# The low part of w_out's first quarter: three products moved from the pooling pass to the wait for the first chunk's softmax weights

## The chip, the core and the metric

The kernel runs on one core of one Trainium2 chip. Its time is the device time of one execution in microseconds (us): three runs of the kernel before took 1018.67, 1019.38 and 1019.65 us, median 1019.38. One more execution was taken with the hardware profiler; every duration below is from that one.

The engines: PE is TensorE's matmul (PEld its weight load), DVE is VectorE, ACT is ScalarE, POOL is GpSimd, SP is SyncE, which issues the DMAs here. Each works through its own list of instructions in the order in which the program wrote them; semaphores hold an instruction until another engine has come far enough. L130 is line 130 of the kernel.

## The reference, cut to what matters

`x` has 12480 rows of 128 channels, `inducing` 32 rows. Inputs are given as 8-byte words; weights are turned into float32 pairs on the chip.

```python
def mab(q, kv):
    s = scale * (q @ kv.T); s = s - s.max(-1)
    a = np.exp(s); a /= a.sum(-1) + 1e-9
    return a @ kv
h = mab(inducing, x)          # pooling: 32 rows attend to all 12480
z = mab(x, h)                 # every row of x attends to the 32
h1 = z @ w_in;  z2 = np.maximum(0.01 * h1, h1) @ w_out          # first feed-forward, 128 -> 2048 -> 128
h2 = z2 @ w2_in               # second feed-forward
g = where(h2 >= 1, h2, where(h2 <= -1, 0, (h2 + 1) ** 2 / 4));  y = g @ w2_out
```

## The kernel before, in words

Nothing sorts the instructions: the order of the calls in the kernel is the order on every engine, and the framework only adds the semaphores that the data and the buffers ask for.

**The pass** (lines 319 to 337) does the pooling over `x` in nine bands with a running maximum. A step `s` has on PE the scores of band `s` (L265), the transposes of the exponentials of band `s-1` (L287), and their products with `x` (L298); DVE takes the maximum (L266, L270) and adds the result up (L302, L312); ACT does the exponentials (L277, L279) and copies the transposed ones (L289). The last two bands have their transposed `x` from memory (`xl`). `warm` (L316) issues products whose results nobody reads: fillers.

**The weights** come as 8-byte words in 512-column quarters. `convert(n, q)` turns quarter `q` of weight `n` (0: w_in, 1: w_out, 2 and 3: the second pair) into float32 in a few steps: L104 on ACT and L105 on DVE, L107, L109 (with L112 on ACT, which writes the high part `whi`), L114. `work(n)` runs `n` such steps, two quarters in turn. The pair of scratch tiles `cva`, `cvb` of a conversion is taken from a pool of three pairs. The low part `wlo` of a w_out quarter is made in one of two ways: on POOL (L121, L122), or, for w_out's quarters 0 and 1 (`PE_LO = 2`), by `low_parts`: three products that add `cva` and `cvb` and subtract `whi` in a PSUM bank (L130, L131, L132), and a copy by ACT (L133). The first two of the three have float32 operands and show as two matmul records each, L132 has fp32r operands and shows as one. `lows` holds what is still to be done; until then the pair of scratch tiles cannot be given to another quarter.

Quarter 0 of w_out is done in step 6 of the pass (L335 and L336), quarter 1 at the third slot of the first chunk (L598). Both read `whi` and their scratch pair, and are wanted by the products of the first chunk (L488).

**Between pass and chunks** (lines 340 to 506) the pooling result `HT` is made (L366), and then the first chunk's attention, one chunk being 480 rows: `attend(0, 0)` scores on PE (L445), `attend(0, 1)` maximum and difference on DVE (L450, L452), 2 exponential on ACT (L455), 3 normalisation on DVE (L459 to L462), 4 the split into a high and a low part (L466 to L469), 5 transposes by products (L475), 6 the copy to `aT` (L480). With them stand `hidden(0, ...)`, which folds `HT` into w_in (L393, L397, L400: `Gs`), conversion steps, and six fillers (L502) in the wait before L475.

**The chunks** (from L509): slot `k` has the product of `aT` with 128 columns of `Gs` (L527), its high and low part (L530, L537), and the three products each with w_out of slot `k-4` (L487 to L489); later the second pair of weights runs five chunks behind. PE is all but gapless from there to the end.

Of the kernel before, what the change touches and what calls it, by code (L numbers as in the profile page):

```python
# [51 lines left out]
NS_B = len(BANDS)  # L52
# [2 lines left out]
         "c0", "w", "w", "w", "w", "w")  # L55
WARM_A = {1: 5, 2: 8}
WARM_B = 4
WARM_T = (3, 4, 4, 5, 6)
WORK_S = ((0, 0), (0, 2), (0, 3), (0, 3), (1, 3), (1, 4), (2, 4), (1, 2), (1, 2))
UNTIL_S = (0, 1, 2, 2, 3, 4, 5, 5, 6)  # L60
WORK_T = (2, 1, 2, 2)
# [7 lines left out]
def moe_kernel(ctx: ExitStack, tc, x_d, xf_d, xl_d, xt_d, it_d, w1_d, w2_d, w3_d, w4_d, y_d):  # L69
# [13 lines left out]
    bank = [ps.tile([128, 512], F32, name=f"bank{i}", tag=f"bank{i}") for i in range(8)]  # L83
# [10 lines left out]
    def convert(n, q):  # L94

        t = raws.pop((n, q))
        up, low = t[:, :, 1], t[:, :, 0]
        sl = slice(q * QW, (q + 1) * QW)  # L100
        a = cv.tile([128, QW], F32, name="cva")
        b = cv.tile([128, QW], F32, name="cvb")
        au, bu = a.bitcast(U32), b.bitcast(U32)
        nc.scalar.activation(a, up.bitcast(F32), AF.Abs, scale=WORD_SCALE)  # L104
        nc.vector.tensor_scalar(out=bu, in0=up.bitcast(U32), scalar1=0x80000000, scalar2=None, op0=ALU.bitwise_and)  # L105
        yield
        nc.vector.scalar_tensor_tensor(out=au, in0=au, scalar=3, in1=bu, op0=ALU.logical_shift_left, op1=ALU.bitwise_or)  # L107
        yield
        nc.vector.tensor_scalar(out=bu, in0=au, scalar1=0xFF800000, scalar2=None, op0=ALU.bitwise_and)  # L109
        if n:  # L110
            hi, lo = whi[n - 1][:, sl], wlo[n - 1][:, sl]
            nc.scalar.activation(hi, a, AF.Copy)  # L112
        yield
        nc.vector.scalar_tensor_tensor(out=b, in0=low.bitcast(U32), scalar=2.0 ** -52, in1=b, op0=ALU.mult, op1=ALU.mult)  # L114
        if n == 0:
            yield
            nc.vector.tensor_tensor(out=w1[:, sl], in0=a, in1=b, op=ALU.add)
        elif n == 1 and q < PE_LO:
            lows.append((bank[2 + q], a, b, hi, lo))
        else:  # L120
            nc.gpsimd.tensor_tensor(out=a, in0=a, in1=hi.bitcast(F32), op=ALU.subtract)  # L121
            nc.gpsimd.tensor_tensor(out=lo, in0=a, in1=b, op=ALU.add)  # L122

    lows = []

    def low_parts(n):

        for _ in range(n):
            s, a, b, hi, lo = lows.pop(0)
            nc.tensor.matmul(s, lhsT=ident, rhs=a, start=True, stop=False)  # L130
            nc.tensor.matmul(s, lhsT=ident, rhs=b, start=False, stop=False)  # L131
            nc.tensor.matmul(s, lhsT=nidentr, rhs=hi, start=False, stop=True)  # L132
            nc.scalar.activation(lo, s, AF.Copy)  # L133
# [5 lines left out]
    def load_next_w():  # L139
        if to_load:  # L140
            load_w(*to_load.pop(0))

    def work(n, until=len(units)):

        for _ in range(n):
            while len(running) < 2 and to_convert and len(units) - len(to_convert) < until:
                running.append((to_convert[0], convert(*to_convert.pop(0))))
            if not running:
                return
            u, r = running.pop(0)  # L150
            if next(r, "end") != "end":
                running.append((u, r))
            else:
                done.add(u)
                if ahead:
                    load_next_w()
# [157 lines left out]
    def warm(n):  # L314
        for _ in range(n):
            nc.tensor.matmul(bank[1][:, :256], lhsT=identr, rhs=twice, start=True, stop=True)  # L316
# [1 line left out]
    denb = const.tile([128, C], F32, name="denb")  # L318
    by_channel(0)
    for s in range(NS_B):  # L320
        ready = len(lows)
        scores(s)
        if s:
            turn(s - 1)
        warm(WARM_A.get(s, 0))
        if s + 1 < NS_B and s + 1 not in xT:
            by_channel(s + 1)
        exps(s)
        work(WORK_S[s][0], UNTIL_S[s])
        if s:  # L330
            gather(s - 1)
            add_up(s - 1)
        if s >= NS_B - XL:
            warm(WARM_B)
        if s == NS_B - 3:  # L335
            low_parts(ready)  # L336
        work(WORK_S[s][1], UNTIL_S[s])


# [3 lines left out]
    turn(NS_B - 1)  # L343
    warm(WARM_T[0])
    mrow = small.tile([1, G4, M], F32, name="mrow")
# [3 lines left out]
    gather(NS_B - 1)  # L349
    warm(WARM_T[1])  # L350
    total(NS_B - 1)
# [9 lines left out]
    nc.tensor.matmul(b_M[:, 384:384 + M], lhsT=R, rhs=fsel, start=True, stop=True)  # L361
    warm(WARM_T[2])
    rden = small.tile([C, M], F32, name="rden")
# [3 lines left out]
                            in1=rden[:, None, :].to_broadcast([C, 3, M]), op=ALU.mult)  # L367
    warm(WARM_T[3])
    inner.close()
# [19 lines left out]
    def hidden(q, part):  # L389

        b = bank[(2, 1, 7, 2)[q]]
        if part == 0:
            nc.tensor.matmul(b[:K1, :], lhsT=HTf, rhs=w1[:, q * 512:(q + 1) * 512], start=True, stop=True)  # L393
            return
        gq = Gs[:, q * 512:(q + 1) * 512]
        if part == 1:
            nc.scalar.activation(gq, b[:K1, :], AF.Copy, scale=1.0 - SLOPE)  # L397
            return
        lo = gq[M:2 * M]
        nc.vector.scalar_tensor_tensor(out=lo, in0=b[M:2 * M, :], scalar=1.0 - SLOPE, in1=lo.bitcast(F32),  # L400
                                       op0=ALU.mult, op1=ALU.subtract)
# [35 lines left out]
    def attend(c, part):  # L437

        b = bX[c % 2]
        if part == 0:  # L440
            t = xts.pop(c)
            if c + 1 < NCH:
                load_xt(c + 1)
            for q in range(CB):
                nc.tensor.matmul(b[:BT, q * M:(q + 1) * M], lhsT=t[:, q * BT:(q + 1) * BT], rhs=HT[:, 0, :],  # L445
                                 start=True, stop=True)
        elif part == 1:
            sv = b[:BT, :CB * M].rearrange("p (b m) -> p b m", m=M)
            m = at.tile([BT, CB], F32, name="m")
            nc.vector.tensor_reduce(out=m, in_=sv, op=ALU.max, axis=AX.X)  # L450
            e = at.tile([BT, CB, M], F32, name="ea")
            nc.vector.tensor_tensor(out=e, in0=sv, in1=m[:, :, None].to_broadcast([BT, CB, M]), op=ALU.subtract)  # L452
            st[c] = e
        elif part == 2:
            nc.scalar.activation(st[c], st[c], AF.Exp, scale=SCALE)  # L455
        elif part == 3:
            e = st[c]
            d = at.tile([BT, CB], F32, name="d")
            nc.vector.tensor_reduce(out=d, in_=e, op=ALU.add, axis=AX.X)  # L459
            nc.vector.tensor_scalar(out=d, in0=d, scalar1=EPS, scalar2=None, op0=ALU.add)  # L460
            nc.vector.reciprocal(out=d, in_=d)
            nc.vector.tensor_tensor(out=e, in0=e, in1=d[:, :, None].to_broadcast([BT, CB, M]), op=ALU.mult)  # L462
        elif part == 4:
            e = st[c]
            s = at.tile([BT, CB, 3, M], F32R, name="s")
            nc.scalar.activation(s[:, :, 1, :], e, AF.Copy)  # L466
            if c == 0:
                nc.scalar.activation(s[:, :, 2, :], e, AF.Copy)
            nc.vector.tensor_tensor(out=s[:, :, 0, :], in0=e, in1=s[:, :, 1, :].bitcast(F32), op=ALU.subtract)  # L469
            st[c] = s  # L470
        elif part == 5:
            s = st.pop(c)
            r = 2 if c else 3
            for q in range(CB):
                nc.tensor.matmul(b[:r * M, q * BT:(q + 1) * BT], lhsT=s[:, q, :r].rearrange("p r m -> p (r m)"),  # L475
                                 rhs=identr[:BT, :BT], start=True, stop=True)
        elif part == 6:
            t = ap.tile([K1, CW], F32R, name="aT")
            r = 2 if c else 3
            nc.scalar.activation(t[:r * M], b[:r * M, :CW], AF.Copy)  # L480
            if c:
                nc.scalar.activation(t[2 * M:], b[M:2 * M, :CW], AF.Copy)
            aT[c] = t
# [14 lines left out]
    attend(0, 3)  # L498
    attend(0, 4)
    hidden(0, 1)  # L500
    hidden(0, 2)
    warm(WARM_T[4])  # L502
    attend(0, 5)
    work(WORK_T[2])
    attend(0, 6)
    work(WORK_T[3])

    NS = NCH * NJ
    for k in range(NS + LAG * NJ + OB + D2):  # L509
# [15 lines left out]
        if in_a:  # L525
            p1 = b1[k % (5 if kb < -2 else 2)][:, :CW]
            nc.tensor.matmul(p1, lhsT=Gs[:, j * 128:(j + 1) * 128], rhs=aT[c], start=True, stop=True)  # L527
            hi = hp1.tile([128, CW], F32R, name="hi1")
            lo = hp1.tile([128, CW], F32R, name="lo1")
# [14 lines left out]
        if kb - 2 in gs:  # L544
            g = gs.pop(kb - 2)
            hi = hp3.tile([128, CW], F32R, name="hi3")
            lo = hp3.tile([128, CW], F32R, name="lo3")
# [19 lines left out]
        if late:  # L567
            lo, g, hi = late
            nc.vector.tensor_tensor(out=lo, in0=g, in1=hi.bitcast(F32), op=ALU.subtract)
        if 0 <= kh < NS:  # L570
# [4 lines left out]
            if jh == NJ - 1:  # L575
                nc.tensor.matmul(px, lhsT=Qs, rhs=aT.pop(ch), start=False, stop=True)  # L576
                hi = x2p.tile([128, CW], F32R, name="x2hi")
                lo = x2p.tile([128, CW], F32R, name="x2lo")
# [14 lines left out]
        if k in HIDDEN:  # L593
            q = 1 + HIDDEN.index(k)
# [58 lines left out]
```

## Time and profile before

| What | Value |
|---|---|
| median of three runs | 1019.38 us (1018.67 to 1019.65) |
| profiled execution, its own time | 1020.59 us |
| span of its trace (first to last instruction) | 1018.8 us |
| PE / DVE / ACT / POOL busy | 98% / 80% / 81% / 63% of the span |
| granted TensorE clock, mean | 0.999 |
| first product of the chunks (L527) starts | 53.08 us |
| last matmul ends | 1015.34 us |

So some 962 us of the 1019 are the chunks, in which PE is busy nearly all the time, and 53 us lie ahead of them. The profiled execution's time is 1.8 us over the span of its trace, and 1.2 us over the median.

A row of the trace reads: start in us, duration in us, engine, line, operation, written tile <- read tiles, shapes, how many; in brackets how long the engine sat idle before it and what ended that. A PE row's end is modelled: it holds some time after the last column, so rows overlap.

### The profile page before, as it was taken

How to read it: one execution, taken by the hardware profiler on the slowest of the kernel's cores; microseconds unless marked ns; L12 is line 12 of the kernel's file. 1: busy time of each engine (PE TensorE's matmuls, PEld its weight loads, DVE VectorE, ACT ScalarE, POOL GpSimd, SP SyncE). 2: the span in 40 equal slices, each digit the busy share in tenths (PEclk: the TensorE clock that was granted, in tenths of full speed). 3: DMA queues.
4: the chain of work that ended last, by engine and by line, in shares of the span. 5: the costliest groups of instructions: out<-in, count | busy, mean ns of one | idle time of the engine just before them, and what ended most of it. 6: DMA issues, size and time to landing. Idle time of an engine off the chain costs nothing.

```text
span 1018.8 us, 15716 instructions
## 1 busy us (share of the span) xinstructions
PE 1001.2 (98%) x5013; PEld 850.6 (83%) x5013; DVE 818.0 (80%) x1494; ACT 828.0 (81%) x1596; POOL 645.5 (63%) x533
## 2 busy tenths in 40 slices
PE   8899999999999999999999999999999999999998
PEld 6567777888888888888888888888888888888887
DVE  4768988777887787877778788777877878789997
ACT  4577778888888888888887888888888788889997
POOL 0034466666666666666666666666676667678886
PEclk9999999999999999999999999999999999999999
DMA  9700000000000000000000000000000000000000
GB/s 348 299 28 20 10 14 7 20 1 20 21 1 20 20 20 1 20 21 1 20 20 1 20 20 20 1 20 20 1 20 21 3 9 11 11 11 11 10 11 21
DMA packets 11523, 29.89 MB, mean 29 GB/s; under 512 B 1408, under 2 KB 8064, under 8 KB 10672
## 3 DMA queue, kind: packets, MB, share of 16 engines
q1 hardware_dynamic: 11440, 28.89, 8.0%
q8 instruction: 39, 0.64, 0.3%
q14 instruction: 44, 0.36, 0.1%
HBM read 22.50 MB, written 6.39 MB: 28 GB/s over the span
## 4 chain that ended last, share of the span: by engine, by line
PE 93%; DVE 4%; ACT 1%; issue 1%; POOL 0%; ACTq 0%; POOLq 0%
PE bank L487 26%; PE bank L488 26%; PE bank L489 26%; PE bank L527 9%; PE bank L445 2%; DVE lo L537 2%; PE bank L253 1%; PE bank L265 1%; PE bank L298 1%; DVE cvb L114 1%; PE bank L576 0%; PE bank L475 0%; PE bank L223 0%; PE bank L316 0%; PE bank L287 0%
## 5 line engine op out<-in xcount | busy, mean ns | idle before, releaser
L553 POOL TENSOR_TENSOR lo<-g,hi 128x480 fp32r<-128x480 f32 x408 | 499.1, 1226 | 235.0 <-PE bank L488 148.5
L530 ACT ACTIVATE hi<-bank 128x480 fp32r<-128x480 f32 x416 | 235.7, 572 | 129.6 <-PE bank L527 127.1
L489 PE MATMUL bank<-lo,whi 128*128 128x480 f32 x832 | 315.6, 379 | 2.1 <-POOL lo L535 2.1
L487 PE MATMUL bank<-hi,whi 128*128 128x480 f32 x832 | 315.9, 380 | 0.0
L488 PE MATMUL bank<-hi,wlo 128*128 128x480 f32 x832 | 315.2, 379 | 0.0
L564 DVE SCALAR_TENSOR_TENSOR g<-bank,sq 128x480 f32<-128x480 f32 x416 | 270.4, 650 | 37.1 <-ACT sq L541 36.7
L541 ACT ACTIVATE sq<-cl,half 128x480 f32<-128x480 f32 x416 | 289.1, 695 | 11.2 <-DVE cl L560 5.4
L537 DVE SCALAR_TENSOR_TENSOR lo<-bank,hi 128x480 fp32r<-128x480 f32 x317 | 205.8, 654 | 109.5 <-ACT hi L530 109.4
L560 DVE TENSOR_SCALAR cl<-bank 128x480 f32<-128x480 f32 x416 | 270.7, 651 | 19.6 <-PE bank L489 13.1
L548 ACT ACTIVATE hi<-g 128x480 fp32r<-128x480 f32 x416 | 248.7, 598 | 0.6 <-DVE g L564 0.5
L489 PEld LDWEIGHTS bank<-lo,whi 128*128 128x128 f32 x832 | 156.0, 188 | 28.8 <-POOL lo L535 3.7
L488 PEld LDWEIGHTS bank<-hi,wlo 128*128 128x128 f32 x832 | 156.6, 188 | 24.4
L487 PEld LDWEIGHTS bank<-hi,whi 128*128 128x128 f32 x832 | 156.3, 188 | 24.5 <-ACT y L589 0.4
L527 PE MATMUL bank<-aT,Gs 96*128 96x480 f32 x416 | 164.4, 396 | 1.8 <-DVE lo L537 1.1
L535 POOL TENSOR_TENSOR lo<-r,hi 128x480 fp32r<-128x480 f32 x99 | 123.8, 1250 | 63.8 <-ACT r L534 60.4
L487 PE MATMUL bank<-x2hi,whi 128*128 128x480 f32 x416 | 159.6, 384 | 0.6 <-DVE g L564 0.6
L488 PE MATMUL bank<-x2hi,wlo 128*128 128x480 f32 x416 | 157.9, 379 | 0.0
L489 PE MATMUL bank<-x2lo,whi 128*128 128x480 f32 x416 | 157.5, 379 | 0.0
L527 PEld LDWEIGHTS bank<-aT,Gs 96*128 96x128 f32 x416 | 78.2, 188 | 15.2 <-DVE lo L537 1.5
L487 PEld LDWEIGHTS bank<-x2hi,whi 128*128 128x128 f32 x416 | 78.8, 190 | 12.7 <-DVE g L564 1.8
L488 PEld LDWEIGHTS bank<-x2hi,wlo 128*128 128x128 f32 x416 | 79.0, 190 | 12.5
L489 PEld LDWEIGHTS bank<-x2lo,whi 128*128 128x128 f32 x416 | 78.1, 188 | 13.0
(115 smaller groups left out, 538.1 us busy)
## 6 DMA issues: line engine op xcount, KB each, us to landing
wraw<-in_w SPq DMA_DIRECT2D x16, 512.0 KB, 9.8
xt<-in_xt SPq DMA_DIRECT2D x26, 240.0 KB, 2.6
out_y<-y SPq DMA_DIRECT2D x26, 240.0 KB, 2.0
xb<-in_x SPq DMA_DIRECT2D x5, 1024.0 KB, 15.6
xl<-in_xl SPq DMA_DIRECT2D x1, 1024.0 KB, 16.6
xb<-in_x SPq DMA_DIRECT2D x2, 256.0 KB, 9.2
xb<-in_x SPq DMA_DIRECT2D x1, 512.0 KB, 4.5
xl<-in_xl SPq DMA_DIRECT2D x1, 256.0 KB, 16.0
```

The lines of the kernel that those rows point to most:

```text
L487: nc.tensor.matmul(out, lhsT=whi[n][:, sl], rhs=hi, start=start, stop=False)
L488: nc.tensor.matmul(out, lhsT=wlo[n][:, sl], rhs=hi, start=False, stop=False)
L489: nc.tensor.matmul(out, lhsT=whi[n][:, sl], rhs=lo, start=False, stop=stop)
L527: nc.tensor.matmul(p1, lhsT=Gs[:, j * 128:(j + 1) * 128], rhs=aT[c], start=True, stop=True)
L530: nc.scalar.activation(hi, p1, AF.Relu)
L535: nc.gpsimd.tensor_tensor(out=lo, in0=r, in1=hi.bitcast(F32), op=ALU.subtract)
L537: nc.vector.scalar_tensor_tensor(out=lo, in0=p1, scalar=0.0, in1=hi.bitcast(F32), op0=ALU.max, op1=ALU.subtract)
L541: nc.scalar.activation(sq, cls.pop(kb - 1), AF.Square, scale=-0.5, bias=half)
L548: nc.scalar.activation(hi, g, AF.Copy)
L553: nc.gpsimd.tensor_tensor(out=lo, in0=g, in1=hi.bitcast(F32), op=ALU.subtract)
L560: nc.vector.tensor_scalar(out=cl, in0=p3, scalar1=1.0, scalar2=-1.0, op0=ALU.min, op1=ALU.max)
L564: nc.vector.scalar_tensor_tensor(out=g, in0=b3[(kb - 1) % 3][:, :CW], scalar=-1.0, in1=sqs.pop(kb - 1), op0=ALU.max, op1=ALU.add)
```

## The change

Four edits. `low_parts` is no longer called in the pass (with it goes `ready`); it is called for one quarter, which is w_out's quarter 0, after `hidden(0, 1)` in the wait for the first chunk's softmax weights. The six fillers that stood there are dropped. The copy `attend(0, 6)` now stands ahead of the two conversion steps `work(WORK_T[2])` and not behind them. And the products go to PSUM bank 3 for both quarters (before: bank 2 for quarter 0), since bank 2 holds `hidden(0, ...)` at the new place.

```diff
-WARM_T = (3, 4, 4, 5, 6)
+WARM_T = (3, 4, 4, 5)
@@ convert
         elif n == 1 and q < PE_LO:
-            lows.append((bank[2 + q], a, b, hi, lo))
+            lows.append((bank[3], a, b, hi, lo))
@@ the pass
     for s in range(NS_B):
-        ready = len(lows)
         scores(s)
...
             warm(WARM_B)
-        if s == NS_B - 3:
-            low_parts(ready)
         work(WORK_S[s][1], UNTIL_S[s])
@@ before the chunks
     hidden(0, 1)
+    low_parts(1)
     hidden(0, 2)
-    warm(WARM_T[4])
     attend(0, 5)
+    attend(0, 6)
     work(WORK_T[2])
-    attend(0, 6)
     work(WORK_T[3])
```

Lines below 335 move up by three: L450 of before is L447 after, L475 is L472, L527 is L524. Names carry their number below, so that a tile can be followed: `cva_300`, `cvb_301` are the scratch pair of w_out's quarter 0, `wraw_139` is the raw quarter 2 of w_out.

On PE, at step 6 of the pass, the three products stand between the products of band 5 (L298) and the scores of band 7 (L265). Before:

```order
L298 MATMUL bank7_88<-xb_119,eT_492 32x128 x15
L130 MATMUL bank2_83<-cva_300,ident_147 128x512
L131 MATMUL bank2_83<-cvb_301,ident_147 128x512
L132 MATMUL bank2_83<-whi0_92,nidentr_157 128x512
L265 MATMUL bank5_86<-xl_127,iT_89 32x512 [waits DMAHW5_49]
```

After, L265 follows L298 there. In the wait, PE has the first chunk's scores, `hidden`, the fillers and the transposes of the weights. Before:

```order
L445 MATMUL bank0_81<-HT_191,xt_135 120x32 x3
L393 MATMUL bank2_83<-w1_91,HT_191 96x512
L316 MATMUL bank1_82<-twice_154,identr_152 128x256 x6
L475 MATMUL bank0_81<-identr_152,s_712 96x120 [waits DVE_49,PE_49,Activation_49]
L475 MATMUL bank0_81<-identr_152,s_712 96x120 x3
```

After:

```order
L442 MATMUL bank0_81<-HT_191,xt_135 120x32 x3
L390 MATMUL bank2_83<-w1_91,HT_191 96x512
L130 MATMUL bank3_84<-cva_300,ident_147 128x512
L131 MATMUL bank3_84<-cvb_301,ident_147 128x512
L132 MATMUL bank3_84<-whi0_92,nidentr_157 128x512
L472 MATMUL bank0_81<-identr_152,s_708 96x120 [waits DVE_49,PE_49,Activation_49]
L472 MATMUL bank0_81<-identr_152,s_708 96x120 x3
```

The three products have taken the fillers' place, behind `hidden`. On DVE, at the same place, stand the end of a conversion (L114), the first step of w_out's quarter 2 (L105), and the first chunk's maximum (L450, after: L447). Before:

```order
L114 SCALAR_TENSOR_TENSOR cvb_586<-wraw_137,cvb_586 128x512
L105 TENSOR_SCALAR cvb_695<-wraw_139 128x512 [waits DMAHW3_49]
L450 TENSOR_REDUCE m_699<-bank0_81 120x4 [waits DMAHW5_49,DMAHW6_49,DMAHW1_49,DMAHW7_49,DMAHW0_49,PE_49]
L452 TENSOR_TENSOR ea_701<-bank0_81,m_699 120x128 [waits DVE_49]
L117 TENSOR_TENSOR w1_91<-cva_585,cvb_586 128x512
```

After:

```order
L114 SCALAR_TENSOR_TENSOR cvb_582<-wraw_137,cvb_582 128x512
L105 TENSOR_SCALAR cvb_691<-wraw_139 128x512 [waits DMAHW3_49,PE_49]
L447 TENSOR_REDUCE m_695<-bank0_81 120x4 [waits DMAHW6_49,DMAHW5_49,DMAHW7_49,DMAHW1_49,DMAHW0_49]
L449 TENSOR_TENSOR ea_697<-bank0_81,m_695 120x128 [waits DVE_49]
L117 TENSOR_TENSOR w1_91<-cva_581,cvb_582 128x512
```

No instruction moves on DVE. The wait on PE has moved from the maximum to L105 ahead of it: in the program after, `cvb_691` lies in the buffer of `cvb_301`, and the semaphore's value there is the one that PE reaches with L131, the last reader of `cvb_301`. In the same way L104 on ACT, which writes `cva_690`, waits for L130. On ACT also, L133 leaves the pass (it stood ahead of L112 of quarter 1) and stands behind L394, and L477 (before: L480) now stands ahead of a conversion's L104. POOL and SP keep their order.

## Rows read from the trace of the kernel before

**Rows 1.** The page: busy share of each engine, and the chain by engine.

```profile
PE 1001.2 (98%) x5013; PEld 850.6 (83%) x5013; DVE 818.0 (80%) x1494; ACT 828.0 (81%) x1596; POOL 645.5 (63%) x533
...
PE 93%; DVE 4%; ACT 1%; issue 1%; POOL 0%; ACTq 0%; POOLq 0%
```

**Rows 2.** The chain of waits in time, steps 6 to 8: start, us, what.

```profile
33.94 1.06 PE bank L130 x2
35.00 0.86 PE bank L131 x2
35.85 0.23 PE bank L132
36.08 1.00 PE bank L265 x8
...
40.51 0.60 PE bank L287 x4
```

**Rows 3.** The timeline of DVE and ACT in the same stretch.

```profile
35.79 0.68 DVE L107 SCALAR_TENSOR_TENSOR cva<-cva,cvb 128x512 uint32<-128x512 uint32 x1
36.50 0.43 DVE L109 TENSOR_SCALAR cvb<-cva 128x512 uint32<-128x512 uint32 x1
36.97 0.69 DVE L114 SCALAR_TENSOR_TENSOR cvb<-wraw,cvb 128x512 f32<-128x512 uint32 x1
37.58 0.68 DVE L266 TENSOR_REDUCE mx<-bank 128x1 f32<-128x512 f32 x1
...
36.12 0.60 ACT L133 ACTIVATE wlo<-bank 128x512 fp32r<-128x512 f32 x1 [0.56 <-PE bank L132]
36.61 0.62 ACT L112 ACTIVATE whi<-cva 128x512 fp32r<-128x512 f32 x1
37.76 0.60 ACT L289 ACTIVATE eT<-bank 128x512 f32<-128x512 f32 x1 [0.53 <-PE bank L287]
38.55 0.69 ACT L277 ACTIVATE e<-bank,nm 128x512 f32<-128x512 f32 x1 [0.19 <-DVE nm L270]
```

**Rows 4.** The timeline of PE in the wait and at the first chunk.

```profile
48.64 1.08 PE L393 MATMUL bank<-w,HT 128*96 128x512 f32 x2
49.16 1.27 PE L316 MATMUL bank<-twice,identr 128*128 128x256 f32 x6
51.82 0.52 PE L475 MATMUL bank<-identr,s 120*96 120x120 f32 x4 [1.39 <-DVE s L469]
53.08 0.48 PE L527 MATMUL bank<-aT,Gs 96*128 96x480 f32 x1 [0.74 <-ACT aT L480]
...
55.56 1.02 PE L393 MATMUL bank<-w,HT 128*96 128x512 f32 x2
56.42 1.02 PE L130 MATMUL bank<-cva,ident 128*128 128x512 f32 x2
57.28 1.02 PE L131 MATMUL bank<-cvb,ident 128*128 128x512 f32 x2
...
60.20 0.46 PE L415 MATMUL bank<-ident,Gs 64*128 64x64 f32 x4 [0.56 <-DVE Gs L400]
```

**Rows 5.** The timeline of DVE in the wait.

```profile
48.40 0.41 DVE L105 TENSOR_SCALAR cvb<-wraw 128x512 uint32<-128x512 uint32 x1
48.84 0.29 DVE L450 TENSOR_REDUCE m<-bank 120x4 f32<-120x128 f32 x1
```

**Rows 6.** The timeline of PE: transposes near the start, and the last matmul.

```profile
10.98 1.91 PE L253 MATMUL bank<-ident,xb 128*128 128x128 f32 x8
...
15.53 1.91 PE L253 MATMUL bank<-ident,xb 128*128 128x128 f32 x16
...
1014.85 0.49 PE L489 MATMUL bank<-lo,whi 128*128 128x480 f32 x1
```

**Rows 7.** Busy time by stretch (us; PE, PEld, DVE, ACT, POOL, then PEclk, DMA, GB/s).

```profile
1015.40:1017.50 2.10, 0.00 (x0) 0.00 (x0) 0.00 (x0) 0.54 (x1) 0.00 (x0) 1.00 0.32 115
1017.60:1018.80 1.20, 0.00 (x0) 0.00 (x0) 0.00 (x0) 0.00 (x0) 0.00 (x0) 0.50 0.00 0
```

## Prediction

> **What bounds the kernel now.** I read the page's shares and its chain first. PE is busy 98% of the span and holds 93% of the chain [rows 1]; its chunks leave no room, so a change ahead of them can only move the moment at which they start, and from there the shift is carried to the end. The question is when the first L527 starts (53.08 us [rows 4]) and whether the stretch behind it runs as before.
>
> I then followed the chain in time. It passes through the three products where they stand now: L130 from 33.94, L131, L132, and only then L265 at 36.08 [rows 2], so 2.14 us of PE lie on it. That looks like the gain. But the timeline of DVE beside it [rows 3] has L107, L109, L114 and L266 from 35.79 to 38.26 with no gap: DVE would let band 7's maximum through no sooner if PE had the scores ready earlier.
>
> Last I read the wait into which the products go. PE's fillers start at 49.16 and PE idles 1.39 us before L475 [rows 4], room in PE for three products. DVE does L105 at 48.40 and the chunk's maximum L450 right behind it at 48.84 [rows 5]. From L450 the softmax of the first chunk runs in one line over DVE and ACT to L475 at 51.82, `aT` and L527.
>
> **The change part by part.** *The products leave the pass.* PE gets 2.14 us free [rows 2]. What keeps the next step: L289 (eT of band 6) now waits for L287 on PE and starts at 37.76 [rows 3]. Without the products, PE has L287 done long before; on ACT, L289 then stands behind L112, and L112 waits for DVE's L107, which ends at 36.47. L112 began at 36.61 because L133 stood ahead; it may begin at 36.51, and the next ACT instruction follows about 0.5 us later (36.12 to 36.61 for L133 and L112 [rows 3]): L289 near 37.05 instead of 37.76, a gain of 0.70. The next guard is L287 of band 7, which needs the exponential at 38.55 + 0.69 = 39.24 [rows 3] and stands at 40.51 [rows 2]: 0.70 sooner is still behind it. So everything up to the wait moves by -0.70. Bounds: nothing if another queue holds the step, 2.14 if DVE makes room too; I take 0.70, worked out from the rows nearest to it.
>
> *The products enter the wait.* They follow `hidden` (L393), which now starts at 48.64 [rows 4], after at 48.64 - 0.70 = 47.94. The same sequence stands in the trace eight us later: L393 at 55.56, L130 at 56.42, L131 at 57.28 and ending 1.02 later [rows 4]. So L393 to the end of L131 is 0.86 + 0.86 + 1.02 = 2.74, and L131 ends at 50.68. Its own time on PE is hidden there: PE would have waited for the weights.
>
> *The wait that this adds.* It is not on PE. L105 of w_out's quarter 2 gets the scratch buffer that quarter 0 still occupies, so by the order of the program after it waits for L131. Behind it in DVE's list stands the chunk's maximum, and behind that the whole softmax. L105 starts at about 50.71 instead of 48.40; with its 0.41 [rows 5], less the 0.08 by which DVE starts the next one early (L114 ends at 37.66, L266 starts at 37.58 [rows 3]), the maximum starts at 51.04 instead of 48.84 [rows 5]: **+2.20 us**, the 0.70 already taken off. ACT's L104 waits for L130 only, ends near 50.5, and is early enough for the exponential. Everything from the maximum to L527 is the same line of work, so L527 starts near 55.28.
>
> *Edits that cost nothing.* L133 takes the place on ACT that L104 had before `aT`; the two are of like length (0.60 for L133 [rows 3]). The L104 moved behind `aT` falls into a wait of ACT for DVE. Bank 3 is read by L133 ahead of `aT` on ACT, without which L527 cannot write there. SP's and POOL's lists are unchanged. If that cover were gone, one ACT instruction, 0.6 us, is the price.
>
> *The fillers go.* PE now idles 1.39 us before L475 and 0.74 before L527 [rows 4], at a granted clock that is full over the whole trace but its end. After the change L132 ends near 50.9 (0.23 behind L131 [rows 2]), L475 starts at 51.82 + 2.20 = 54.02: 3.1 us without a matmul, then 0.52 us of work, then 0.7 idle. In the trace the last matmul ends at 1015.34 [rows 6], the granted clock is 1.00 up to 1017.5 and 0.50 from 1017.6 [rows 7]: 2.2 us after the last matmul it fell from 2.4 to 1.2 GHz. I therefore expect it to fall here too. The price: near the start 8 transposes take the 1.91 us in which 16 go a little later [rows 6], which I read as the low level and the high one, so PE works at half speed at the low one. The change of rate lies between 10.98 and 15.53, so at most 4.6 us of work at the low level; that much at half speed loses 2.3 us, of which PE's wait of 0.56 for DVE before L415 [rows 4] absorbs some: 1.7. The other end is 0. No row lies nearer to one of them, so I take the middle, **+0.9**.
>
> The Trainium skill, "TensorE: Matmul & The Clock Gate", section "What's actually happening", says that the low rate is the default and activity releases it. By it taking the fillers out speaks against this change; by that rule the sum is +3.1, and without it +2.2. The trace agrees at its end (0.50 after the last matmul).
>
> **Sum.** -0.70 and the added wait give +2.20; the clock +0.9: +3.1 us. On the profiled execution: span 1018.8 + 3.1 = 1021.9, its own time 1020.59 + 3.1 = 1023.7. On the median of the runs: 1019.38 + 3.1 = **1022.5 us**.
>
> **Rivals.**
> *A. The clock holds.* The gap is broken by L475, and gaps of 1.39 us leave it full now. Then only the wait counts: 1019.38 + 2.2 = 1021.6. Against it stands the fall after 2.2 us [rows 7].
> *B. The clock falls earlier and for longer.* In the pass, with L265 ending near 35.0 and L287 near 35.6, PE waits for eT until 37.7, about 2.1 us; the fall at the end came after as much. The low level then lasts through steps 7 and 8, where PE is on the chain, and again in the wait: twice the 1.7 or more, 1019.38 + 2.2 + 3.4 = 1025.0. For it: the length of the gap; against it: dense work on both sides.
> *C. The pass gives back the whole 2.14.* The place is DVE in step 6: if L266 of band 7 is not held by L107 to L114, L265 moves by 2.14, and the maximum starts 1.44 us earlier than I say. With the clock full that is 1019.38 + 2.20 - 1.44 = 1020.1, no change that can be told. It decides from a gain of 0.9 in the pass on. For it: the chain runs through PE there [rows 2]. Against it: DVE's gapless rows [rows 3].
> *D. The wait at L105 costs nothing*, since the maximum is not held: then the change gives -0.70 to -2.14, 1018.7 to 1017.2. That needs the order of DVE's list to be another than the program's; I see nothing for it.
>
> **How the numbers follow.** About 0.2% (2.04 us) is what a measurement of this kernel can tell from no change; the bounds are 1017.34 and 1021.42. Forecast 0.54, A 0.30, B 0.07, C 0.06, D 0.03. Slower: nearly all of the forecast (0.50), a good half of A (0.17), B: 0.74. Same: the rest of the forecast (0.04) and of A (0.13), and most of C (0.05): 0.22. Faster: D and what is left of C, 0.04. The range has A's lower side (+1.6, if the pass gives 1.3) and the forecast with its clock at the full 1.7 (+3.9), widened for part of B: 1020.9 to 1024.4.
>
> **What would show it.** In the profile after: L105 on DVE starting near 50.7, its idle time ended by PE's L131; the maximum near 51.0; L527 near 55.3; L289 of band 6 near 37.05; L415 at 62.4 with a full clock, near 63.3 without; a granted clock of 0.50 somewhere from 53 to 60. The forecast is wrong if the maximum starts before 50, if L289 of step 6 moves by over 0.9, or, in the clock's term, if the granted clock stays at 1.00.

## The result and the profile after

| | before | after |
|---|---|---|
| median of four runs | 1019.51 us (1018.67 to 1020.46) | 1024.77 us (1023.44 to 1027.43) |
| after / before | | 1.0052 [1.0037, 1.0067] |
| profiled execution, its own time | 1020.59 us | 1027.43 us |
| span of its trace | 1018.8 us | 1025.6 us |
| granted clock, mean | 0.999 | 0.993 |

The kernel is slower by 5.3 us on the medians, where 3.1 were forecast; the time lies above the range. The profiled execution of after is the slowest of its four runs: it stands 6.8 us over that of before, 1.6 us more than the medians differ. Where those lie is told below.

The page of after, busy shares and the chain by engine, which answers to [rows 1]:

```profile
PE 1005.5 (98%) x5007; PEld 853.5 (83%) x5007; DVE 817.2 (80%) x1494; ACT 828.1 (81%) x1596; POOL 645.8 (63%) x533
...
PE 92%; DVE 5%; ACT 2%; issue 1%; POOL 0%; DMA 0%; ACTq 0%; POOLq 0%; SPq 0%
```

PE has six matmuls fewer (the fillers) and is busy for 4.3 us longer. The same products took more time, which points at the clock and not at a wait. DVE and ACT are where they were. The span grew by 6.8 us, more than those 4.3, so two things must be looked for: a lower clock, and a wait.

The timeline of after at step 6 of the pass (all engines), which answers to [rows 2, 3]:

```profile
34.84 0.66 PE L287 MATMUL bank<-ident,e 128*128 128x128 f32 x4
...
36.47 0.63 ACT L112 ACTIVATE whi<-cva 128x512 fp32r<-128x512 f32 x1 [0.94 <-DVE cva L107]
...
37.01 0.58 ACT L289 ACTIVATE eT<-bank 128x512 f32<-128x512 f32 x1
37.54 0.68 DVE L266 TENSOR_REDUCE mx<-bank 128x1 f32<-128x512 f32 x1
37.64 1.34 PEld L298 LDWEIGHTS bank<-xb,eT 128*32 128x32 f32 x32 [2.39 <-ACT eT L289]
37.64 1.79 PE L298 MATMUL bank<-xb,eT 128*32 128x128 f32 x32 [2.15 <-DVE cvb L114]
```

L289 starts at 37.01 (before: 37.76), held by L112 as the prediction had it. But PE, with nothing left to do until that copy, idles 2.15 us. (The weight load of L298 names L289, whose result it reads. The bracket of the matmul itself names DVE's L114; L298 reads nothing of it, and releasers are inferred.)

The timeline of after in the wait, which answers to [rows 4, 5]:

```profile
51.12 1.02 PE L131 MATMUL bank<-cvb,ident 128*128 128x512 f32 x2
...
51.33 0.67 ACT L104 ACTIVATE cva<-wraw 128x512 f32<-128x512 f32 x1 [4.78 <-PE bank L130]
...
51.58 0.80 PE L132 MATMUL bank<-whi,nidentr 128*128 128x512 f32 x1
52.18 0.43 DVE L105 TENSOR_SCALAR cvb<-wraw 128x512 uint32<-128x512 uint32 x1 [3.00 <-PE bank L131]
52.53 0.28 DVE L447 TENSOR_REDUCE m<-bank 120x4 f32<-120x128 f32 x1
...
55.49 0.87 PE L472 MATMUL bank<-identr,s 120*96 120x120 f32 x4 [3.11 <-DVE s L466]
...
57.01 0.77 PE L524 MATMUL bank<-aT,Gs 96*128 96x480 f32 x1 [0.66 <-ACT aT L477]
...
61.77 1.02 PE L390 MATMUL bank<-w,HT 128*96 128x512 f32 x2
...
65.76 0.46 PE L412 MATMUL bank<-ident,Gs 64*128 64x64 f32 x4
```

L105 has idled 3.00 us for L131, the maximum (L447) stands at 52.53 instead of 48.84, and PE idles 3.11 us before L472. L472 and L524 each take about 1.6 times as long as before (0.87 and 0.77 for 0.52 and 0.48). L412 has lost the 0.56 us for which PE waited before it.

Busy time by stretch in after (columns as in [rows 7]):

```profile
34.43:37.80 3.37, 1.16 (x16) 0.58 (x16) 3.30 (x9) 2.22 (x6) 0.00 (x0) 1.00 1.02 405
37.90:41.20 3.30, 3.30 (x45) 2.31 (x36) 0.97 (x4) 0.96 (x3) 0.00 (x0) 0.50 1.02 408
41.30:54.90 13.60, 9.57 (x87) 6.78 (x86) 7.63 (x27) 3.44 (x10) 0.00 (x0) 1.00 0.32 113
55.00:61.70 6.70, 5.56 (x11) 2.96 (x12) 5.09 (x10) 4.41 (x11) 1.42 (x2) 0.50 0.01 2
61.80:66.00 4.20, 4.20 (x16) 2.27 (x15) 3.71 (x7) 3.10 (x7) 2.76 (x3) 1.00 0.00 0
...
167.60:170.90 3.30, 3.30 (x10) 2.67 (x10) 2.17 (x5) 2.47 (x5) 3.15 (x3) 0.50 0.02 5
```

The clock was granted at 1.2 GHz in three stretches, where the column shows none but the end in the trace of before: behind the new gap in the pass, behind the new gap in the wait, and at 167.6. In the first PE was busy throughout (3.30 of 3.30): work at half speed, on the chain.

### The profile page after: what moved, and what is told of

Same layout as the page of the kernel before. It is cut to its first block, busy times and chain, and to the rows that moved or that the text cites. A ratio compares the mean times of both kernels' runs of the same rounds, so it can differ in the third digit from the quotient of the medians.

```text
span 1025.6 us, 15705 instructions
## 1 busy us (share of the span) xinstructions
PE 1005.5 (98%) x5007; PEld 853.5 (83%) x5007; DVE 817.2 (80%) x1494; ACT 828.1 (81%) x1596; POOL 645.8 (63%) x533
## 4 chain that ended last, share of the span: by engine, by line
PE 92%; DVE 5%; ACT 2%; issue 1%; POOL 0%; DMA 0%; ACTq 0%; POOLq 0%; SPq 0%
PE bank L484 26%; PE bank L485 25%; PE bank L486 25%; PE bank L524 9%; PE bank L442 2%; DVE lo L534 1%; PE bank L253 1%; DVE cvb L114 1%; ACT hi L527 1%; PE bank L472 1%; PE bank L265 1%; PE bank L573 0%; PE bank L298 0%; PE bank L223 0%; DVE cva L107 0%
## 5 line engine op out<-in xcount | busy, mean ns | idle before, releaser
L527 ACT ACTIVATE hi<-bank 128x480 fp32r<-128x480 f32 x416 | 236.0, 573 | 130.2 <-PE bank L524 127.7
L524 PE MATMUL bank<-aT,Gs 96*128 96x480 f32 x416 | 166.0, 400 | 1.7 <-DVE lo L534 1.1
L524 PEld LDWEIGHTS bank<-aT,Gs 96*128 96x128 f32 x416 | 78.7, 189 | 15.8 <-DVE lo L534 1.5
```

The lines of the kernel that those rows point to most:

```text
L527: nc.scalar.activation(hi, p1, AF.Relu)
```

## The experiments

The theory after the result was that of the prediction, with the fall in the pass that it had put down as rival B: L105's wait costs 2.2 us, and the gap in the pass and the gap in the wait each cost a fall of the clock. Against it stood that the wait alone makes the loss and the falls are absorbed, and that the loss comes from the products' new place itself (bank 3, the new order on ACT). What each run was to show is quoted with it.

Executions of one kernel differ in the first 25 us, so all times of the traces are counted from one event that the change does not touch, the start of eT of band 4 (the fifth L289). This table, worked out from the traces so, is what the verdicts go by (us; the last column in us from the span's start):

```
kernel                eT4    eT6   L105   max   first  L415/  chunk 1  granted clock 0.50
                                               L527   L412           (ahead of the end)
before               28.01   9.75  20.39  20.84  25.07  32.19  46.64   none
after                27.98   9.03  24.20  24.55  29.03  37.78  52.23   37.9-41.3, 54.9-61.7, 167.6-171.0
e1 both gaps filled  28.07   9.02  22.72  23.06  27.23  34.39  50.36   65.3-68.7
e2 wait filled       25.11   9.03  24.20  24.55  28.70  35.87  50.32   35.1-38.6
e5 pass filled       26.50   9.02  22.71  23.06  27.21  36.71  51.16   8.8-12.2, 53.1-60.0
e3 four pairs        28.14   9.03  21.14  21.58  25.74  32.91  47.37   38.2-41.6
e4 four, pass filled 26.50   9.03  19.66  20.11  24.27  31.44  45.90   8.6-12.0
e6 after again       26.55   9.02  24.20  24.55  29.03  37.75  52.20   9.0-12.5, 36.3-39.8, 53.4-60.2, 166.1-169.5
e7 before, no filler 26.55   9.75  20.39  20.83  25.31  34.17  48.62   9.0-12.5, 50.0-56.8, 162.6-166.1
e8 before, swap      28.13   9.75  20.39  20.83  24.97  32.17  46.61   none
e9 as e4             26.50   9.03  19.66  20.10  24.27  31.44  45.89   8.6-12.1, 158.8-162.2
e10 as e4, start     25.44   9.03  19.66  20.10  24.27  31.44  45.91   157.7-161.1
```

(eT4 from the span's start, the others from eT4. L412 of after is L415 of before, L524 is L527; max is L447 or L450; chunk 1 is the first product of the second chunk, as they count from 0.) Each row is from one trace; the other runs give a time and a mean granted clock each.

**e1: fillers in both gaps of after.**

```diff
-WARM_A = {1: 5, 2: 8}
+WARM_A = {1: 5, 2: 8, 7: 16}
     low_parts(1)
+    warm(24)
```

> The changed kernel with 16 fillers more in the pass (behind the transposes of band 6) and 24 behind the three products in the wait, so that PE's two new gaps are filled and nothing else moves. Theory (the loss has two parts, L105's wait for L131 and the low clock that follows PE's two gaps): the granted clock stays at 1.00 from 30 to 66 us, L289 of band 6 near 37.0, the maximum L447 near 51.0, L412 near 62.4; time about 2.2 us over the kernel before (2.0 to 2.6). Rival (the wait is the whole loss, and the low clock only lies in time that PE has to spare): about 5 us over before, as the changed kernel.

Measured: 1022.2 us (12 runs), 1.0022 [1.0011, 1.0034] of before, which is 1.1 to 3.5 us and not the rival's 5; the medians themselves differ by 3.1. Timelines of e1 on PE and DVE in the wait:

```profile
50.79 0.43 DVE L105 TENSOR_SCALAR cvb<-wraw 128x512 uint32<-128x512 uint32 x1 [3.00 <-PE bank L131]
51.13 0.28 DVE L447 TENSOR_REDUCE m<-bank 120x4 f32<-120x128 f32 x1
...
54.09 0.52 PE L472 MATMUL bank<-identr,s 120*96 120x120 f32 x4 [0.25 <-DVE s L466]
...
62.46 0.46 PE L412 MATMUL bank<-ident,Gs 64*128 64x64 f32 x4 [0.62 <-DVE Gs L397]
```

And its stretches:

```profile
34.60:53.00 18.40, 16.59 (x174) 13.17 (x171) 11.68 (x38) 6.38 (x18) 0.00 (x0) 1.00 0.60 226
53.00:65.30 12.30, 10.75 (x52) 6.95 (x51) 10.36 (x18) 9.56 (x21) 6.15 (x5) 1.00 0.00 0
65.40:68.70 3.30, 3.30 (x11) 2.30 (x10) 1.90 (x5) 1.50 (x4) 0.31 (x1) 0.50 0.26 74
```

With the clock full from 34.6 to 65.3, all that is left of the change at L412 is 34.39 - 32.19 = 2.20 us: the wait at L105, at the very size that the prediction gave it (+2.20, the pass's 0.7 taken off). L472 is back at 0.52 and the idle 0.6 before L412 is back too. The fall at 65.3 was expected by nobody; behind it chunk 1 is 3.7 us late in this execution. It comes after a stretch in which PE was busy 10.75 of 12.30 us. The trace of e2 has the same fillers in the wait and no fall there, so what brings it is open.

**e2: only the wait filled. e5: only the pass filled.** Each is one half of e1's diff: e2 has the `warm(24)`, e5 the `7: 16`.

> The changed kernel with the 24 fillers in the wait only; PE's gap of 2.1 us in the pass stays. Theory: the clock falls behind the gap in the pass in the profiled run as in the changed kernel's, so L447 near 52.5, but it stays full behind the wait: L412 near 63.8; time 2.2 to 3.8 us over before, depending on how often the fall in the pass comes. Rival (the fall behind the wait costs nothing): about 5 us over before.

> The changed kernel with the 16 fillers in the pass only; PE's gap of 3.1 us in the wait stays. Theory (a gap of this length is followed by the low clock whenever it comes, and costs by itself): counted from the copy eT of band 4 the maximum L447 is where it was with both gaps filled (2.2 us later than before), but the clock falls to 0.50 near 53 to 56, and L412 is 3.5 to 4.5 us later than before, not 2.2; time 3.5 to 5 us over before. Rival (only the fall in the pass costs; in the wait DVE hides it): L412 2.2 us later than before and the time 2 to 3 us over it.

Measured: e2 1021.69 us (12 runs), 1.0025 [1.0012, 1.0037]; e5 1023.35 us (7 runs), 1.0038 [1.0024, 1.0051]. The stretches of e2:

```profile
35.20:38.50 3.30, 3.30 (x38) 2.31 (x31) 1.08 (x5) 0.96 (x3) 0.00 (x0) 0.50 1.04 412
38.60:64.00 25.40, 22.40 (x155) 16.11 (x154) 17.41 (x43) 13.01 (x30) 6.32 (x5) 1.00 0.29 107
```

And of e5:

```profile
34.00:53.10 19.10, 14.18 (x151) 10.54 (x150) 11.62 (x37) 6.76 (x20) 0.00 (x0) 1.00 0.63 239
53.20:59.90 6.70, 6.19 (x9) 2.88 (x10) 5.78 (x11) 4.70 (x9) 2.82 (x2) 0.50 0.01 2
```

In the traces each has the fall behind the gap that it leaves open and loses the other. The pair separates the two prices. In the pass: the maximum stands at 24.55 with the fall (after, e2, e6) and at 23.06 without it (e1, e5): **1.49 us**. In the wait: from the maximum to L412 it is 11.33 in e1, 11.32 in e2 and 11.35 in before, but 13.65 in e5 and 13.23 in after: **1.9 to 2.3 us**.

The 1.49 us are the price where the fall comes, and it does not come in every run. The medians do not show it: e2 stands 0.5 us under e1, which has the pass filled. The 3.4 us of low clock take 0.0017 off a run's mean granted clock, and four of e2's twelve runs stand at 0.999 (1020.02 to 1020.45 us), which leaves no room for them. The fall in the wait takes 0.0033; six of e5's seven runs, at 0.993 to 0.997, have room for it, and only the fastest (1021.27 us, 0.998) has not.

**e3: a fourth pair of scratch buffers. e4: that, and the pass filled. e9: e4 once more, beside e10.**

```diff
-    cv = fill.enter_context(tc.tile_pool(name="cv", bufs=3, side="right"))
+    cv = fill.enter_context(tc.tile_pool(name="cv", bufs=4, side="right"))
```

e4 and e9 have `7: 16` in `WARM_A` as well.

> The changed kernel with four scratch pairs for the conversions in place of three, so that quarter 2 of w_out gets a pair of its own and L105 waits for no product; no fillers added. Theory: L105 starts behind L114 again, PE goes from L132 to L472 without a long gap, so only the gap in the pass is left. With the clock falling there, L447 near 49.6 and the time 0 to 1.5 us over before; without, 48.1 and 0.7 us under before. Rival (the products' time on PE, not L105's wait, delays the softmax): the maximum stays near 51 to 52.5, and the time 3 us or more over before.

> Four scratch pairs and the 16 fillers in the pass. Theory: neither the wait nor the low clock is left; what remains of the change is the 0.7 us that the pass gives back: L289 of band 6 near 37.05, L447 near 48.1, L524 first near 52.3, the clock at 1.00 from 30 to 60 us, and the time 0.7 us under before (0.4 to 1.0). Rival (the pass gives back nothing, as its gain is lost later): the same as before within 0.2 us. Rival (the pass gives back all of the 2.14 us of PE): 2 us under before.

> Four scratch pairs and the 16 fillers in the pass once more, unaltered, for more executions. Theory: 0.75 us under before, as its trace showed from eT of band 4 to the end; the median 0.3 to 1.2 us under before. Rival (the 0.75 us are lost to a later fall of the clock): within 0.2 us of before.

Measured: e3 1018.6 us, 0.9992 [0.9980, 1.0004]; e4 1018.4 us, 0.9995 [0.9984, 1.0005]; e9 1019.47 us, 0.9993 [0.9981, 1.0005], twelve runs each. None can be told from before by its time. The traces can. DVE of e4 in the wait:

```profile
45.56 0.67 DVE L114 SCALAR_TENSOR_TENSOR cvb<-wraw,cvb 128x512 f32<-128x512 uint32 x1
46.16 0.41 DVE L105 TENSOR_SCALAR cvb<-wraw 128x512 uint32<-128x512 uint32 x1
46.60 0.29 DVE L447 TENSOR_REDUCE m<-bank 120x4 f32<-120x128 f32 x1
```

L105 follows L114 with no bracket behind it: with a buffer of its own it waits for no one, and the products stand on PE where they stand in after. So it was the buffer that made the wait, and not the products' place, their bank or the order on ACT. That the new place itself costs something falls with it. From eT4 on, e4 and e9 run 0.75 us ahead of before at L412 and at chunk 1, which is what the pass gives back and nothing more. In e4 the lead is there at the last matmul too; in e9's trace a fall at 158.8 has taken it back by then. e3, without the fillers in the pass, has its fall (38.2 to 41.6) and pays 1.47 for it (L412 at 32.91 instead of 31.44). But its trace is of the slowest of its twelve runs: three others (1016.96 to 1017.47 us) have a mean clock of 0.999 or 1.000, with no room for that fall, and e3's median, 0.5 us under before, lies between the 0 to 1.5 over that was expected with the fall and the 0.7 under without it.

**e6: after once more.** No edit.

> The changed kernel once more, unaltered, for a second profile and a time beside the other kernels of this chip. Theory (the wait 2.2, the fall in the pass 1.5, that in the wait 1.5 to 2): falls at both gaps again, L412 5 to 6 us later than before counted from eT of band 4, and the time 4.5 to 6 us over before. Rival (the first profile showed an unlucky execution): one of the two falls is missing, and the time is 2 to 4 us over before.

Measured: 1024.92 us (5 runs), 1.0054 [1.0040, 1.0067]. Its own start is another one (eT4 at 26.55, not 27.98), and from there every time up to L412 agrees with the first trace of after within 0.03 us, the two falls included. The nine runs of after, four at the result and five here, have a mean clock of 0.991 to 0.994, where none of the 82 runs of before beside the experiments is under 0.996. So the falls belong to the kernel and not to one unlucky execution, though a mean does not tell which fall a run had.

**e7: before without the six fillers.**

```diff
-WARM_T = (3, 4, 4, 5, 6)
+WARM_T = (3, 4, 4, 5, 0)
```

> The kernel before without the six fillers in the wait (the fillers' removal alone). PE's gap before L475 grows from 1.4 to about 2.1 us. Theory (a gap of that length is enough, as the one of 2.15 us in the pass was): the maximum and the first L527 stay where they are, the clock falls near 55, and L415 comes 1 to 2 us later in the profile; time 0.5 to 2 us over before. Rival (the gap is broken up by L475 and the clock holds): no difference, within 0.2%.

Measured: 1020.63 us (11 runs), 1.0018 [1.0007, 1.0029]. PE of e7 behind the gap:

```profile
50.34 0.86 PE L475 MATMUL bank<-identr,s 120*96 120x120 f32 x4 [2.09 <-DVE s L469]
```

And its stretches:

```profile
34.00:49.90 15.90, 12.00 (x140) 8.05 (x138) 11.05 (x35) 6.27 (x18) 0.00 (x0) 1.00 0.68 258
50.10:56.80 6.70, 5.80 (x12) 3.13 (x13) 5.14 (x10) 4.16 (x8) 1.82 (x2) 0.50 0.10 36
```

Nothing but the fillers is gone, the gap grows from 1.39 to 2.09 us, and the clock falls for as long as in after. L415 is 1.98 us late. All eleven runs have a mean clock of 0.997 or less, with room for this fall. So the price of the fillers stands by itself, without the products or the wait, and here a gap of 2.1 us was enough for it.

**e8: before with only the copy and the conversion steps exchanged** (`attend(0, 6)` ahead of `work(WORK_T[2])`).

> The kernel before with the copy to aT ahead of the two conversion steps (that edit alone). Theory (the edit costs nothing and frees nothing that lies on the way): counted from eT of band 4, the first L527 comes up to 0.5 us sooner, as aT no longer stands behind a conversion's L104 on ACT, and L415 within 0.1 us of before; time the same. Rival (it delays the conversion of w_out's quarter 3 enough to stall): L415 or the second chunk 0.3 us or more later.

Measured: 1019.73 us (8 runs, one of them of 3300.93 us, which is left out of the ratio and which nothing here explains), 0.9994 [0.9984, 1.0005]. L527 is 0.10 sooner and L415 0.02: nothing, as the prediction's step on the free edits said of the copy's place.

**e10: e9, with fillers at the pass's start.**

```diff
+WARM_S = {0: 2, 1: 4}
-    def warm(n):
+    def warm(n, to=1):
-            nc.tensor.matmul(bank[1][:, :256], lhsT=identr, rhs=twice, start=True, stop=True)
+            nc.tensor.matmul(bank[to][:, :256], lhsT=identr, rhs=twice, start=True, stop=True)
     for s in range(NS_B):
+        warm(WARM_S.get(s, 0), 3)
         scores(s)
```

> The same with six fillers more near the start, two ahead of the scores of band 0 and four ahead of those of band 1, where PE waits 0.4 and 0.8 us for copies. Theory (the executions of one kernel differ because the clock rises at another moment in the start, 4 to 14 us, and the gaps there push it down again or keep it down): eT of band 4 near 25 to 26.5 in more executions, the median 0.5 to 2 us under that without them. Rival (the rise does not depend on these gaps): the same median within 0.5 us, and the same spread.

Measured: 1017.72 us (1016.94 to 1019.06, 11 runs), 0.9979 [0.9970, 0.9987] of before: it beats both kernels, before by 2.1 us. Of these, 0.75 are the pass's, with the wait bought off by the fourth pair; what is left would be the start's. PE of e9 near the start:

```profile
9.57 1.91 PE L253 MATMUL bank<-ident,xb 128*128 128x128 f32 x8
```

The same eight transposes in e10 (its lines are one further down):

```profile
6.51 0.72 PE L317 MATMUL bank<-twice,identr 128*128 128x256 f32 x4
...
8.62 1.04 PE L254 MATMUL bank<-ident,xb 128*128 128x128 f32 x8
```

At full rate they take 1.04 instead of 1.91, and eT4 is at 25.44 instead of 26.50. The runs of e10 spread over 2.1 us, those of e9 over 4.4 and of before beside them over 3.5. Only the fillers differ between e9 and e10, and the medians are 1.75 us apart, so they are the likely cause; it is not shown. The intervals of the two overlap, and the one trace of each does not decide it: e2, without these fillers, started just as early (eT4 at 25.11, the same eight transposes in 1.04).

## Why the prediction was wrong

The direction and the wait's term were right; the clock's terms were not. At L412, where the shift is complete, after stands 37.78 - 32.19 = 5.59 us later than before. The three measured parts follow one another (up to the maximum without the fall, what the fall adds there, and from the maximum to L412), so they add up by themselves; that each is what its row calls it is shown by the runs named in the row. The first row is contained in the second:

| step of the prediction | said | measured | by |
|---|---|---|---|
| products leave the pass (in the next row) | -0.70 | -0.72 | eT6 9.75 to 9.03, in each kernel that has the edit |
| the wait at L105, the pass's part taken off | +2.20 | +2.22 | e1, e5: maximum at 23.06, before 20.84 |
| the fall in the pass | 0 (rival B alone) | +1.49 | maximum at 24.55 or 23.06 |
| the fall in the wait | +0.9 | +1.88 | maximum to L412, 13.23 or 11.35 (e1, e2: 11.33, 11.32) |
| the edits that cost nothing | 0 | 0 | e8 for the copy; e4, which has them all and is ahead by what the pass gives back |
| sum at L412 | +3.1 | +5.59 | |

*The wait.* Right in place, cause and size: L105 idles for L131, and a fourth buffer takes it away (e4). The absolute times, 52.18 for L105 and not 50.7, are off by the fall ahead of it alone; e1 has it at 50.79.

*The fillers go.* The step that failed, first in its size. The fall came, after a gap as long as the 3.1 us worked out. I put its price between 0 and 1.7 and took the middle. The 1.7 came from work "at most 4.6 us" at the low level between two rows of the start [rows 6]. Those rows bound the moment at which the rate rose, not how long a low stretch lasts: PE had been at the low rate since its first products. This row of PE in before has 20 transposes at about the rate of those eight:

```profile
1.36 4.53 PE L223 MATMUL bank<-ident 128*128 128x128 f32 x20 [1.36 <-POOL ident masks.py:199]
```

The low stretch of the wait lasted 6.8 us, and it holds 4.7 us of gapless work behind the first L524 alone (57.01 to 61.74): half of that is 2.37, less the 0.56 of slack 1.8. The softmax's own PE parts, L472 and L524, add 0.24, since the line from the maximum to the first L524 is 4.48 instead of 4.24. That makes 2.05 against 1.88 measured. The bound taken from the start was too low, and within its bounds the middle was no better than a guess.

*The fall in the pass.* The other half of the same failure, and the larger one. The prediction saw the gap in its rival B, and gave it 2.1 us; it is 2.15. It gave the rival a chance of 0.07, since dense work stands on both sides. That reason did not hold: the clock fell behind the gap in every trace that has it (after, e2, e3, e6), and in the dense work that followed it cost 1.49 of the 1.7 that one fall was priced at there. The only row at hand for a gap of this length was the fall at the end, 2.2 us after the last matmul [rows 7], and I used it for the wait and argued it away for the pass. Rival B's time, 1025.0, is the measured one within 0.3 us. Its mechanism is the one that the runs show, but the closeness is in part luck: it has 1.7 for each fall, one price too high and the other too low (1.49 and 1.88).

The Trainium skill, "TensorE: Matmul & The Clock Gate", section "What's actually happening", has activity release the low rate, and the prediction weighed that rule for one of the two gaps. The trace of after agrees at both (0.50 from 37.9 and from 54.9). The rule should have been put to each stretch that loses work on PE, the one that the products leave included.

*What is left.* The profiled execution lost 6.8 us up to its last matmul (994.16 - 987.33, both from eT4). Beyond the 5.59, a third fall at 167.6 cost 1.5 there (from chunk 5's first product to chunk 6's it is 29.84 instead of 28.30). It follows gaps that before has too, of the same 1.07 and 0.65 us (at 160.11 and 161.24). PE of after ahead of it:

```profile
165.31 0.48 PE L524 MATMUL bank<-aT,Gs 96*128 96x480 f32 x1 [1.07 <-DVE lo L534]
...
166.44 0.48 PE L484 MATMUL bank<-x2hi,whi 128*128 128x480 f32 x1 [0.65 <-DVE g L561]
```

The fall is there in the traces of after, e6, e7, e9 and e10 and absent in those of before, e1 to e5 and e8. e4 and e9 are the same kernel, one without it and one with it, so it does not need the change; whether the change makes it more frequent is not shown. The remaining -0.3 lies between chunk 2 and chunk 4, and the second trace of after (e6) does not have it; what makes it is open.

## What to carry to other kernels

Before work is moved off an engine's list, look at both ends of the move: what the place it leaves has left to do (here a gap of 2.15 us, whose price, where the fall came, was twice the 0.72 gained), and what its scratch buffers' next users are queued ahead of (here DVE's L105 in front of the softmax, 2.2 us). If one row of the trace shows a price for a gap, apply it to every gap of that length, and bound the price by the work that actually stands behind each one. Count small shifts in the trace from an event that the change leaves alone: e4's 0.75 us can be seen there, and not in the times. And look at the other runs before one trace is taken for the kernel: each of their mean clocks says whether a fall had room.

## What the runs showed of the hardware

- Gaps on PE of 2.09 (e7), 2.15 (after, e2, e3, e6) and 3.11 us (after, e5, e6) were each followed by a granted clock of 0.50, in every trace that has them; the 1.39 us of before and 1.38 of e8 were not. In the runs without a trace it is not so every time: by their mean clock, at least four of twelve of e2 and three of twelve of e3 had no fall behind the 2.15 us.
- In after the clock was low from 37.9 to 41.3 behind the gap in the pass, from 54.9 to 61.7 behind the one in the wait, and in e7 and e5 for the same 6.8 us.
- It also fell without a single long gap: in e1 at 65.3, where PE was busy 10.75 of the 12.3 us before, and near 160, behind gaps of 1.07 and 0.65 us, in some executions of one kernel and not in others (e9, e4). Which executions, no run here tells.
- In the first microseconds the column of the granted clock read 1.00 in before, while eight transposes took the 1.91 us of sixteen [rows 6]. There the durations are to be believed, and the column is not. eT4 came at 25.1 to 28.1 us over the twelve traces, in step with the first 20 transposes: 4.53 us where it came at 28.0 to 28.1, 4.25 to 4.46 at 26.5 to 26.6, 3.72 and 3.87 at 25.4 and 25.1. These 3.0 us are nearly the 3.5 over which the runs of before beside e9 spread; that they make this spread is not shown, since falls further on add to it.
